# One kernel, one change: overflow rows of a block fetched one block ahead instead of two, held by a copy, and scattered when the block is closed

## The chip, the cores and the metric

The kernel runs on 1 core of one Trainium2 chip. The metric is the device time of one execution in microseconds (us). Before the change it is 3940.48 us, the median of 3 runs (3938.98 to 3941.68).

## The reference

A graph of 10000 nodes and 160000 edges, 128 features a node. Seven hops of a normalized sparse sum, then one small attention block over the eight tokens of each node:

```python
h = x                                            # (10000, 128)
toks = [x]
for _ in range(7):
    msg = h[src] * deg_inv_sqrt[src, None] * deg_inv_sqrt[dst, None]
    h = segment_sum(msg, dst, N)                 # sum over the edges into each node
    toks.append(h)
tok = stack(toks, axis=1)                        # (N, 8, D)
...                                              # layernorm, q/k/v, softmax, wo, layernorm, readout
```

The change touches only the hops.

## The kernel before, in words

The destination nodes lie in 79 blocks of 128. One hop is 79 blocks in a fixed order (the list `order`), and the hops follow each other. The table of the last hop's values, split in two f16 halves, lies on the chip (`tab`, 128 partitions by 80 by 256) and, row by row, in memory as well (`tabd` the whole table, `tabh` the last rows of it). For each block a tile `w` of zeros and ones in fp8 says which edge takes which source row and which destination it adds to. It is made once, in hop 1, and in hops 2 to 7 loaded from memory for every block.

A block of hops 2 to 7 works in three steps on TensorE (PE):

- *Gather* (line 608): 72 small matmuls with 128x32 weights out of `w` pick source rows out of `tab` into PSUM. They go in nine pairs of eight, each pair into one PSUM tile `p`, of which there are six. Each pair is then scaled by 4 and copied to an f16 tile `eb`, by ScalarE (ACT, line 613) for pairs 0, 2, 4, 5, 7 and by VectorE (DVE, line 615) for pairs 1, 3, 6, 8. This is called an evacuation below.
- *Scatter* (line 583, `scat`): 18 matmuls with 128x128 weights out of `w` add the nine `eb` tiles into the block's accumulator `acc`.
- Two more matmuls add rows that the gather does not hold. `og[n][0]` are 128 rows of `tabh` (the last group), `og[n][1]` are *overflow rows*, up to 128 edges that found no place in the cells of `w`; their destinations are in `Sov`. Both are brought from memory by an indirect DMA that GpSimd (POOL) issues (`fetch`, line 544). `begin` opens the accumulator with them (line 568), after the nine gathers of the block.

The matmuls of a block are not issued all at once. `pend` holds scatters that wait, with a lag of two: in block n, after the gathers and `begin`, PE does the last two scatters of block n-1, then the close of block n-1, and then the first seven scatters of block n. `close` reduces the accumulator on DVE (`s`, line 599), ACT and DVE then write the block's row of the next table (`entries`, lines 644 to 646), POOL scales the block's token (`r`, line 653), and the sync engine stores both.

The first two blocks of a hop cannot have their overflow rows when they begin, because those may come from any row of the table that the last hop has just finished. They are `late`: `begin` leaves the overflow matmul out, and `close` does it (line 597), behind the block's last scatter.

`ahead(n)` issues fetches from block n. In the normal case it is called just behind the block's first pair: it fetches `og[n+2][0]`, and this fetch is held by a one-column copy from that pair's `eb` tile to `og` (line 543), so that it doesn't start earlier; then it fetches `og[n+2][1]`, which has no copy of its own. At n = 0 the overflow rows of blocks 0, 1 and 2 are fetched together, at n = 1 those of block 3. Each of the two `og` tags has three buffers.

Of the kernel before, what the change touches and what calls it, by code (L numbers as in the profile page):

```python
# [19 lines left out]
NT = 79  # L20
NG = 18
NI = 1
# [25 lines left out]
class Hops:  # L48
# [608 lines left out]
    def run(self, ctx, att, nhop=K):  # L657
        tc, nc, V, A, T, G = self.tc, self.nc, self.nc.vector, self.nc.scalar, self.nc.tensor, self.nc.gpsimd
        with ExitStack() as c:
# [11 lines left out]
            pend = []  # L671
# [54 lines left out]
        with ExitStack() as c:  # L726
            lp = c.enter_context(tc.tile_pool(name="lp2", bufs=1))
            self.mx[0], self.ctok[1] = (lp.tile([128, NT], F32, name=z) for z in ("mx0", "ctok1"))
            self.c1 = [lp.tile([128, NT], F32, name=f"c1{i}") for i in range(2)]
            self.gsp = c.enter_context(tc.tile_pool(name="gs2", bufs=5))  # L730
            self.pg = c.enter_context(tc.tile_pool(name="pg2", bufs=6, space=PSUM))
            self.pacc = c.enter_context(tc.tile_pool(name="pc2", bufs=2, space=PSUM))
            self.ogp = c.enter_context(tc.tile_pool(name="og2", bufs=3))
            self.fp = c.enter_context(tc.tile_pool(name="fp2", bufs=4))
            self.sp = c.enter_context(tc.tile_pool(name="sp2", bufs=2))
            self.more_ebufs(c.enter_context(tc.tile_pool(name="eb2", bufs=1)), 9, False)
            pend = []
            for k in range(2, nhop + 1):
                i = 1 - k % 2
                tab, din = self.tab[i], (self.tabd[i], self.tabh[i])  # L740
                ct = self.ctok[i]
                last = k == nhop
                V.tensor_scalar(ct, self.disT, self.sinv, None, op0=ALU.mult)


                def scale(part, n, i=i, k=k):
                    if part == 0 and n == 0 and k == 2:
                        self.count()
                    if part != 1 - n:
                        return  # L750
                    if n == 0:
                        mc = self.sp.tile([128, 1], F32, name="mc")
                        V.tensor_reduce(mc, self.mx[i], axis=X, op=ALU.max)
                        scale.m = self.colmax(self.pg, self.sp, mc, "p")
                        V.tensor_mul(scale.m, scale.m, self.rho)
                    else:
                        q = self.pow2_of(self.pg, self.sp, scale.m, 2.0 ** 8, "p")
                        V.tensor_mul(self.sinv, self.sinv, q[:, 1:2])
                        V.tensor_scalar(self.c1[i], self.dis2, q[:, 0:1], None, op0=ALU.mult)

                def fin(t, s, acc, k=k, ct=ct, last=last, i=i):
                    if not last:
                        self.entries(t, s, i)
                        self.rows(1 - i, self.tab[1 - i], t, t + 1, nc.sync)
                    self.token_out(k, t, s, ct)


                order = [*range(4 * NG, NT), *range(4 * NG)]
                og = [[None] * (NI + 1) for _ in order]


                def ahead(n, after=None, og=og, order=order, din=din):
                    if n + 2 < NT:
                        for j in range(NI):
                            og[n + 2][j] = self.fetch(order[n + 2], j, din, after=None if j else after)
                    for m in range(0 if n == 0 else n + 2, min(n + 3, NT) if n >= 0 else 0):
                        og[m][NI] = self.fetch(order[m], NI, din, "ogl" if m < 2 else None)

                ahead(-2)
                ahead(-1)  # L780
                for n, t in enumerate(order):
                    w = self.gsp.tile([128, (NJ + NG) * 128], F8, name="w")
                    nc.sync.dma_start(w, self.GSd[t])
                    if k == 2 and n == 20:
                        att.constants(c, self.pg.tile([128, 512], F32, name="aw", tag="p"), self.ident)
                    if last and 40 <= n < 40 + 8 * FIRST:
                        att.load((n - 40) // 8, (n % 8,))

                    after = pend.pop() if n == 1 else None
                    for _ in self.block(t, w, tab, og[n], pend, 2, (9,), False, lambda jj: jj in (0, 2, 4, 5, 7), fin, n == 0, n < 2,  # L790
                                        (lambda part, n=n: scale(part, n)) if n < 2 and not last else None,
                                        lambda after=None, n=n: ahead(n, after), after):
                        pass
                while pend:
                    pend.pop(0)()
# [578 lines left out]
```

## Time and profile before

| | before |
|---|---|
| time, median of 3 runs | 3940.48 us |
| time of the profiled execution | 3935.55 us |
| its span, first to last instruction | 3933.8 us |
| mean granted TensorE clock | 0.977 |
| PE busy | 3693.9 us (94%) |
| DVE busy | 3172.3 us (81%) |
| ACT busy | 2812.9 us (72%) |
| POOL busy | 1678.8 us (43%) |

The profiled execution is 4.9 us under the median, and 1.75 us of it lie outside the span. Hops 2 to 7 lie from about 1170 us to 3282 us of the span.

How to read it: a row of the timeline gives the start in us, the busy time in us, the engine, the line, the operation, the tiles as out<-in, and how many instructions are merged (x). In square brackets stands the idle time of the engine just before it, and what ended that idle time. A matmul's start is recorded and its end is modelled, so an engine that waits for a matmul's result can wait longer than the matmul's row says. A row of the windows gives the stretch, its length, and then the busy time (and number of instructions) of PE, PE's weight loads, DVE, ACT and POOL in it, the granted clock, the DMA share and GB/s.

### The profile page before, as it was taken

Reading aid. Unit: us, or ns where it says so; the run is one execution under the profiler, and the core shown is the slowest. Engines: PE = TensorE matmul, PEld = TensorE weight load, DVE = VectorE, ACT = ScalarE, POOL = GpSimd, SP = SyncE. Lnnn points to the kernel's source line nnn. Section 1 sums busy time; section 2 is a strip of 40 time slices with the busy share of each in tenths; the row PEclk is TensorE's granted clock in tenths of the full one; section 3 lists DMA queues with packets and bytes.
Section 4 is the critical chain, followed back from the end, with each engine's and each line's share of the span. In section 5 each row is a group of like instructions: output and inputs, shape, how many; then the busy total and the mean of one; then the engine's idle time right before and its main releaser. Section 6 shows DMA issues by size and latency. Waiting matters only on the chain.

```text
span 3933.8 us, 174231 instructions
## 1 busy us (share of the span) xinstructions
PE 3693.9 (94%) x74141; PEld 2983.6 (76%) x74141; DVE 3172.3 (81%) x6888; ACT 2812.9 (72%) x6950; POOL 1678.8 (43%) x2221
## 2 busy tenths in 40 slices
PE   6786899999989999999999999999999998999997
PEld 4665677777768888888788788888878886777775
DVE  8998999999967777777777777777776664888888
ACT  6885577777766666766666667666765667888885
POOL 0000233323236665666666566656656662121111
PEclk8898899999999999999999999999999999999998
DMA  3100454544546666666666666666666552222220
GB/s 101 38 2 1 140 168 154 163 152 161 161 150 202 202 199 194 204 199 204 188 201 201 192 201 203 198 192 199 204 192 201 187 187 92 82 77 85 77 83 19
DMA packets 332729, 595.58 MB, mean 151 GB/s; under 512 B 57447, under 2 KB 215493, under 8 KB 326693
## 3 DMA queue, kind: packets, MB, share of 16 engines
q1 hardware_dynamic: 293989, 506.70, 40.0%
q0 software_dynamic: 35392, 72.55, 6.5%
q8 instruction: 580, 9.50, 1.0%
q10 hardware_dynamic: 2560, 5.12, 0.5%
q14 instruction: 208, 1.70, 0.1%
HBM read 455.49 MB, written 128.67 MB: 148 GB/s over the span
## 4 chain that ended last, share of the span: by engine, by line
PE 75%; DVE 14%; ACT 4%; DMA 4%; issue 2%; SPq 0%; another core or an unknown queue 0%; ACTq 0%; DVEq 0%; POOLq 0%
PE p L608 27%; PE acc L583 23%; PE acc L568 4%; PE pv L1018 4%; PE pu L1002 3%; DVE ux L226 2%; DVE o L219 2%; PE po L1037 2%; PE pt L992 2%; DVE oh L213 2%; PE tb L449 2%; DVE w L532 2%; PE ps L1067 1%; DVE R L219 1%; PE acc L558 1%
## 5 line engine op out<-in xcount | busy, mean ns | idle before, releaser
L613 ACT ACTIVATE eb<-p 128x512 f16<-128x512 f32 x3065 | 1638.7, 603 | 571.0 <-PE p L608 339.1
L615 DVE TENSOR_TENSOR eb<-p,four 128x512 f16<-128x512 f32 x1912 | 1230.9, 685 | 327.5 <-PE acc L583 189.7
L608 PE MATMUL p<-tab,w 128*32 128x256 f16 x39816 | 1291.8, 274 | 39.4 <-ACT eb L613 17.4
L608 PEld LDWEIGHTS <-w 128*32 128x32 fp8e4 x39816 | 997.5, 96 | 223.8 <-issue 169.2
L583 PE MATMUL acc<-eb,w 128*128 128x256 f16 x8532 | 1014.2, 273 | 0.5 <-issue 0.3
L583 PEld LDWEIGHTS <-w 128*128 128x128 fp8e4 x8532 | 836.9, 98 | 99.8 <-issue 1.0
L544 POOL DMA_INDIRECT og<-tabh,oidx x553 | 616.9, 1115 | 655.2 <-DVE oidx L468 394.5
L544 POOL DMA_INDIRECT og<-tabd,oidx x541 | 551.8, 1020 | 739.1 <-PE acc L566 359.6
L653 POOL TENSOR_SCALAR r<-s,ctok 128x128 f32<-128x128 f32 x474 | 294.8, 622 | 44.8 <-DVE s L599 27.8
L644 ACT ACTIVATE tab<-s,c 128x128 f16<-128x128 f32 x395 | 158.5, 401 | 198.0 <-DVE eb L615 171.4
L645 DVE SCALAR_TENSOR_TENSOR tab<-s,c,tab 128x128 f16<-128x128 f32 x395 | 138.9, 352 | 180.9 <-issue 168.3
L1107 POOL TENSOR_TENSOR p<-e,in 128x1024 f32<-128x1024 f32 (+1 forms) x40 | 76.5, 1914 | 446.6 <-DVE e L1106 446.6
L1059 ACT ACTIVATE junk<-tab 128x128 f32<-128x128 f32 x626 | 248.4, 401 | 8.2 <-SPq L1343 6.8
L347 ACT ACTIVATE rs<-iof,rb 128x128 fp8e4<-128x128 f32 x784 | 231.8, 391 | 0.3
L558 PE MATMUL acc<-eb,w 128*128 128x129 f16 x1422 | 214.2, 223 | 1.0 <-ACT w L529 0.9
L532 DVE TENSOR_TENSOR w<-dsl,iof 128x2432 fp8e4<-128x2432 f16 x79 | 211.9, 2682 | 2.7 <-PE acc L559 2.7
L599 DVE TENSOR_REDUCE s<-acc 128x128 f32<-128x256 f32 x474 | 196.3, 414 | 19.9 <-issue 8.9
L559 PE MATMUL acc<-eb,w 128*128 128x128 f16 x1422 | 210.1, 220 | 0.0
L543 POOL COPY og<-eb 128x1 f16<-128x1 f16 x452 | 84.0, 186 | 254.3 <-ACT eb L613 254.3
L558 PEld LDWEIGHTS <-w 128*128 128x128 fp8e4 x1501 | 139.2, 98 | 68.0 <-issue 64.3
L1018 PEld LDWEIGHTS pv<-Wv,xT 128*64 128x64 f32 x2504 | 138.8, 137 | 44.4 <-ACT uT L1003 29.7
L1018 PE MATMUL pv<-Wv,xT 128*64 128x131 f32 x2504 | 163.1, 280 | 8.6 <-issue 3.9
(299 smaller groups left out, 5033.1 us busy)
## 6 DMA issues: line engine op xcount, KB each, us to landing
w<-gsd SPq DMA_DIRECT2D x474, 592.0 KB
gsd<-w SPq DMA_DIRECT2D x79, 592.0 KB
tok<-r SPq DMA_DIRECT2D x546, 64.0 KB
tab<-tok SPq DMA_DIRECT2D x273, 128.0 KB
tabd<-tab SPq DMA_DIRECT2D x396, 64.0 KB
ra<-srow SPq DMA_DIRECT2D x79, 320.0 KB
rb<-srow SPq DMA_DIRECT2D x79, 256.0 KB
og<-tabh,oidx POOLq DMA_INDIRECT x553
```

The costliest lines, as they stand in the source:

```text
L347: A.activation(ro[:, j - a, i, :], self.iof, AF.Abs_reciprocal_sqrt, scale=2.0 ** 21, bias=rb[:, j - VP, i:i + 1], saturate=False)
L532: V.tensor_tensor(w[:, :NJ * 128].rearrange("p (j d) -> p j d", d=128), dsl[:, g, :, None].to_broadcast([128, NJ, 128]), self.iof1[:, None ...
L544: self.nc.gpsimd.indirect_dma_start(out=o, out_offset=None, in_=src[0] if i == NI else src[1], in_offset=bass.IndirectOffsetOnAxis(ap=self ...
L558: T.matmul(acc[0][:, :128 + ones], W, rows[:, 128:256 + ones], start=start, stop=False, skip_group_check=True)
L559: T.matmul(acc[0][:, :128], W, rows[:, :128], start=False, stop=False, skip_group_check=True)
L583: T.matmul(acc[0][:, :256], w[:, J * 128:(J + 1) * 128], e[:, j, :256], start=False, stop=J == NG - 1 and not late)
L608: T.matmul(p[32 * q:32 * q + 32, j], w[:, NJ * 128 + s * CAP:NJ * 128 + (s + 1) * CAP], tab[:, s, :], start=True, stop=True)
L613: A.activation(e[:, :n, 0:256], pv, AF.Copy, scale=4.0)
L615: V.tensor_tensor(e[:, :n, 0:256], pv, self.four[:, :, None].to_broadcast([128, n, 256]), op=ALU.mult)
L653: self.nc.gpsimd.tensor_scalar(r, s, ct[:, t:t + 1], None, op0=ALU.mult)
L1018: T.matmul(p[64 * h:64 * h + 64, u - us[0], :], S[i]["xT"][:, h * m + q, 64 * c:64 * c + 64], Wv, start=True, stop=True, tile_position=(0, ...
L1059: A.activation(j, S[i]["x"][:, g, :], AF.Square, bias=S[i]["x"][:, g, 0:1], scale=-1.0, accum_out=R[i % 6][:, 0, g:g + 1])
```

## The change

In hops 2 to 7 every block is now `late`: its overflow matmul stands in `close` and no longer in `begin`. The overflow rows of block n+1 are fetched in `ahead(n)`, from block 2 on, one block ahead and not two. This fetch too is held by a one-column copy of the block's first pair. At n = 0 the first three blocks' rows are fetched as before; at n = 1 no overflow rows are fetched.

```diff
                     if n + 2 < NT:
                         for j in range(NI):
                             og[n + 2][j] = self.fetch(order[n + 2], j, din, after=None if j else after)
-                    for m in range(0 if n == 0 else n + 2, min(n + 3, NT) if n >= 0 else 0):
-                        og[m][NI] = self.fetch(order[m], NI, din, "ogl" if m < 2 else None)
+                    if n == 0:
+                        for m in range(3):
+                            og[m][NI] = self.fetch(order[m], NI, din, "ogl" if m < 2 else None)
+                    elif 1 < n < NT - 1:
+                        og[n + 1][NI] = self.fetch(order[n + 1], NI, din, after=after)
...
-                    for _ in self.block(t, w, tab, og[n], pend, 2, (9,), False, lambda jj: jj in (0, 2, 4, 5, 7), fin, n == 0, n < 2,
+                    for _ in self.block(t, w, tab, og[n], pend, 2, (9,), False, lambda jj: jj in (0, 2, 4, 5, 7), fin, n == 0, True,
```

What this does to the order of the instructions shows on two engines. On PE, in a block in the middle of hop 2 (`og` the fetched rows, `Sov` the overflow destinations, `acc` the accumulators):

```order
 L568 LDWEIGHTS w
 L568 MATMUL acc<-og_24898,w 128x256
-L568 LDWEIGHTS Sov
-L568 MATMUL acc<-og_24901,Sov 128x256
 L583 LDWEIGHTS w
 L583 MATMUL acc<-eb_260,w 128x256
...
 L583 LDWEIGHTS w
 L583 MATMUL acc<-eb_262,w 128x256
+L597 LDWEIGHTS Sov
+L597 MATMUL acc<-og_24901,Sov 128x256
 L583 LDWEIGHTS w
 L583 MATMUL acc<-eb_264,w 128x256
```

The same weights and the same matmul stand four scatter matmuls later, for the block before, between the last scatter of that block and the first of the next. The number of instructions on PE is the same.

On POOL, two blocks in the middle of a hop, before (`og0` the last group's rows, `og1` the overflow rows, `r` the token):

```order
L543 COPY og0_43527<-eb12_24215 128x1
L544 DMA og0_43527<-tabh0_168,oidx_255 128x256
L544 DMA og1_43657<-tabd0_166,oidx_255 128x256
L653 TENSOR_SCALAR r_43625<-s_43619,ctok0_250 128x128
L543 COPY og0_43654<-eb7_24210 128x1
L544 DMA og0_43654<-tabh0_168,oidx_255 128x256
L544 DMA og1_43784<-tabd0_166,oidx_255 128x256
L653 TENSOR_SCALAR r_43752<-s_43746,ctok0_250 128x128
```

The scheduler that writes the order has moved the overflow fetch forward by a block: `og1_43657` is used by the same block as `og0_43654`, but its fetch stands one block earlier, beside that of `og0_43527`. It waits there for the buffer that the overflow matmul of the block in work gives back, so in fact overflow rows are asked for three blocks ahead.

Two such blocks in the changed kernel:

```order
L543 COPY og0_40342<-eb2_260 128x1
L543 COPY og1_40345<-eb2_260 128x1
L544 DMA og0_40342<-tabh0_168,oidx_255 128x256
L544 DMA og1_40345<-tabd0_166,oidx_255 128x256
L653 TENSOR_SCALAR r_40441<-s_40435,ctok0_250 128x128
L543 COPY og0_40470<-eb11_24214 128x1
L543 COPY og1_40473<-eb11_24214 128x1
L544 DMA og0_40470<-tabh0_168,oidx_255 128x256
L544 DMA og1_40473<-tabd0_166,oidx_255 128x256
L653 TENSOR_SCALAR r_40569<-s_40563,ctok0_250 128x128
```

Both copies stand ahead of both fetches, and the fetches follow each other with nothing between them. The copy of `og1` has taken over its fetch's wait for the buffer, which is now that of the block two before; the fetches wait only for their copies. POOL has 456 instructions more, one copy in each of 76 blocks of six hops.

On POOL at the start of hop 3, before (`ogl` the overflow rows of blocks 0 and 1):

```order
L544 DMA og0_34585<-tabh0_168,oidx_255 128x256
L544 DMA ogl_34452<-tabd0_166,oidx_255 128x256
L544 DMA ogl_34454<-tabd0_166,oidx_255 128x256
L544 DMA og1_34456<-tabd0_166,oidx_255 128x256
L544 DMA og1_34587<-tabd0_166,oidx_255 128x256
L544 DMA og1_34633<-tabd0_166,oidx_255 128x256
L653 TENSOR_SCALAR r_34615<-s_34608,ctok0_250 128x128
L543 COPY og0_34630<-eb12_24215 128x1
L544 DMA og0_34630<-tabh0_168,oidx_255 128x256
```

And in the changed kernel:

```order
L544 DMA og0_34661<-tabh0_168,oidx_255 128x256
L544 DMA ogl_34528<-tabd0_166,oidx_255 128x256
L544 DMA ogl_34530<-tabd0_166,oidx_255 128x256
L544 DMA og1_34532<-tabd0_166,oidx_255 128x256
L653 TENSOR_SCALAR r_34689<-s_34682,ctok0_250 128x128
L543 COPY og0_34704<-eb12_24215 128x1
L543 COPY og1_34707<-eb12_24215 128x1
L544 DMA og0_34704<-tabh0_168,oidx_255 128x256
L544 DMA og1_34707<-tabd0_166,oidx_255 128x256
```

Where five fetches from `tabd` stood in a row there are three; the other two now stand behind copies of block 2 and of block 3. On DVE and ACT the order is the same in both kernels.

## The prediction

> **What bounds the kernel now.** The page's first part was read first.
>
> ```profile
> PE 3693.9 (94%) x74141; PEld 2983.6 (76%) x74141; DVE 3172.3 (81%) x6888; ACT 2812.9 (72%) x6950; POOL 1678.8 (43%) x2221
> ```
>
> PE is busy 94% of the span, so next comes the timeline of one block in the middle of hop 4, to see whether anything but PE ends a block.
>
> ```profile
> 1800.94 2.15 PE L608 MATMUL p<-tab,w 128*32 128x256 f16 x72
> 1801.45 2.06 ACT L613 ACTIVATE eb<-p 128x512 f16<-128x512 f32 x4 [0.35 <-PE p L608]
> 1802.11 0.18 POOL L543 COPY og<-eb 128x1 f16<-128x1 f16 x1 [0.55 <-ACT eb L613]
> 1802.57 1.02 POOL L544 DMA_INDIRECT og<-tabh,oidx  x1 [0.27 <-POOL og L543]
> 1803.02 0.28 PE L568 MATMUL acc<-og,w 128*128 128x256 f16 x1
> 1803.14 0.27 PE L568 MATMUL acc<-og,Sov 128*128 128x256 f16 x1
> 1803.25 2.13 PE L583 MATMUL acc<-eb,w 128*128 128x256 f16 x18
> 1803.98 0.60 ACT L613 ACTIVATE eb<-p 128x512 f16<-128x512 f32 x1 [0.46 <-PE acc L583]
> 1804.01 0.69 DVE L615 TENSOR_TENSOR eb<-p,four 128x512 f16<-128x512 f32 x1 [0.45 <-PE acc L583]
> 1804.32 0.95 POOL L544 DMA_INDIRECT og<-tabd,oidx  x1 [0.72 <-PE acc L583]
> 1804.62 0.41 DVE L599 TENSOR_REDUCE s<-acc 128x128 f32<-128x256 f32 x1
> 1805.07 0.40 ACT L644 ACTIVATE tab<-s,c 128x128 f16<-128x128 f32 x1 [0.49 <-DVE eb L615]
> 1805.30 0.62 POOL L653 TENSOR_SCALAR r<-s,ctok 128x128 f32<-128x128 f32 x1
> 1805.31 2.15 PE L608 MATMUL p<-tab,w 128*32 128x256 f16 x72
> 1805.50 0.35 DVE L645 SCALAR_TENSOR_TENSOR tab<-s,c,tab 128x128 f16<-128x128 f32 x1 [0.47 <-issue]
> 1806.05 1.89 DVE L615 TENSOR_TENSOR eb<-p,four 128x512 f16<-128x512 f32 x3
> ```
>
> The block runs from 1800.94 to 1805.31, 4.37 us, and PE has no bracket in it: it never waits. Call the start T. Two evacuations, the eighth on ACT (T+3.04) and the ninth on DVE (T+3.07), come late: all 72 gathers ended at 1803.09 by their row, T+2.15, and both engines were idle 0.46 and 0.45 us. The name in the bracket, a scatter matmul, isn't what they need. What lies over that time on another engine is the `tabh` fetch on POOL, T+1.63 to T+2.65. The waits over hops 2 to 7 say that this is the rule:
>
> ```profile
> ACT eb L613 <- PE acc L583: 189.5, 406, 0.8
> DVE eb L615 <- PE acc L583: 188.6, 418, 0.8
> ```
>
> Some 410 of 474 blocks show it, with 0.46 us each. I read it so: while POOL issues an indirect fetch, and 0.3 to 0.4 us beyond, a matmul's signal reaches ACT and DVE late. PE itself goes on; it suffers only when its six buffers `p` are full. That point is near: the ninth evacuation, the reduce (T+3.68), lines 644 and 645 and then the next block's first DVE evacuation stand in one queue. The latter starts at 1806.05 and its first of three takes a third of 1.89, so it ends near 1806.7; the next block's eighth pair, which reuses its buffer, starts at 1805.31 plus seven ninths of 2.15, 1806.98. With the signal's way back the slack is 0.1 to 0.25 us.
>
> The Trainium skill speaks against my reading: "SBUF — State Buffer", section "Who interferes with whom", says that only the port pair which VectorE and GpSimd share causes contention, and that TensorE and ScalarE never wait on anyone. The row of 406 waits on ACT does not look so; what the time would be by that rule is the last rival.
>
> The blocks that are longer stand at the hops' starts. The windows of the third block of hops 3 to 7 (length, PE, PE loads, DVE, ACT, POOL, clock, DMA share, GB/s), with a normal block ahead:
>
> ```profile
> 1800.94:1805.31 4.37, 4.37 (x95) 3.71 (x94) 3.45 (x7) 3.07 (x7) 2.79 (x5) 1.00 0.65 200
> 1527.11:1533.21 6.10, 5.22 (x94) 3.83 (x93) 3.69 (x8) 3.33 (x7) 3.49 (x5) 1.00 0.33 73
> 1876.13:1887.57 11.44, 8.48 (x94) 5.24 (x93) 4.33 (x10) 3.35 (x7) 5.71 (x8) 0.70 0.43 124
> 2231.62:2239.78 8.16, 5.88 (x95) 3.96 (x95) 4.39 (x10) 3.35 (x7) 5.16 (x7) 1.00 0.37 104
> 2584.23:2594.21 9.98, 7.20 (x95) 4.68 (x95) 4.42 (x10) 3.24 (x7) 5.76 (x8) 0.83 0.49 145
> 2941.01:2947.73 6.72, 6.28 (x94) 4.30 (x93) 3.52 (x6) 2.88 (x5) 4.97 (x8) 0.75 0.24 65
> ```
>
> Over 4.37 us they lose 1.73, 7.07, 3.79, 5.61 and 2.35, together 20.6 us. The timeline of hop 4 shows why:
>
> ```profile
> 1873.16 0.95 POOL L544 DMA_INDIRECT ogl<-tabd,oidx  x1 [2.43 <-DMA tabd<-tab]
> 1875.94 0.27 PE L597 MATMUL acc<-ogl,Sov 128*128 128x256 f16 x1
> 1878.16 0.94 POOL L544 DMA_INDIRECT og<-tabd,oidx  x1 [0.30 <-issue]
> 1881.77 0.69 DVE L615 TENSOR_TENSOR eb<-p,four 128x512 f16<-128x512 f32 x1 [4.65 <-remote]
> ```
>
> Five fetches start between 1873.16 and 1878.16, 1.25 us apart, and DVE is idle 4.65 us until 1881.77, after gathers that had long run.
>
> **The change part by part.** *The moved matmul.* One matmul of the overflow form, 1803.02 to 1803.14, so 0.11 us from start to start, moves four scatters later on PE. The sum for PE is zero. The close now holds it, but it was ahead of the close before too, so the reduce's input is ready at the same time. Nothing covers this; nothing needs to.
>
> *When the rows must be there.* The fetch now starts near T+3.1 and its matmul stands after two blocks, the gathers, line 568 and four scatters: 2×4.37 + 2.08 + 5×0.11 = T+11.4, 8.3 us later. The first fetch of hop 4 started at 1873.16 and its rows were used at 1875.94, so 2.8 us do. Cost zero, unless a fetch takes three times that. What is queued behind the new copy on POOL is both fetches and the token `r`; for `r` waits only the sync engine's store, and nobody on PE.
>
> *The second copy.* 456 copies of 0.18 us. POOL works 2.79 us of 4.37 us in the windows row, so its own time is covered. But both copies stand ahead of both fetches, so the `tabh` fetch moves from T+1.63 by 0 to 0.24 us (the lower end if the 0.27 us ahead of it covers the copy, the upper with 0.06 us for the step between two); I take 0.18, T+1.81. The eighth pair's signal is then due before the hold begins and its evacuation is on time.
>
> *The second fetch.* Before, it waited 0.72 us for a buffer that the block's own overflow matmul gives back, T+3.38. Now that wait has been met long ago (the buffer is that of two blocks before), so it starts 0.30 us behind the first, T+3.13: back to back in each block. The close's last matmul is issued near T+2.6, its signal due at T+2.8 or so, inside the first fetch's hold. The nearest rows are the few blocks of before in which the two fetches happen to stand so:
>
> ```profile
> 1535.39 1.02 POOL L544 DMA_INDIRECT og<-tabh,oidx  x1 [0.51 <-POOL og L543]
> 1536.72 0.96 POOL L544 DMA_INDIRECT og<-tabd,oidx  x1 [0.30 <-PE acc L583]
> 1536.76 0.42 DVE L599 TENSOR_REDUCE s<-acc 128x128 f32<-128x256 f32 x1 [0.21 <-PE acc L583]
> ...
> 1539.77 1.02 POOL L544 DMA_INDIRECT og<-tabh,oidx  x1 [0.51 <-POOL og L543]
> 1541.10 0.95 POOL L544 DMA_INDIRECT og<-tabd,oidx  x1 [0.30 <-issue]
> 1541.81 0.42 DVE L599 TENSOR_REDUCE s<-acc 128x128 f32<-128x256 f32 x1 [0.75 <-PE acc L583]
> ```
>
> In the first the reduce starts 1.37 us after the first fetch, in the second 2.04 us. From T+1.81 that gives the reduce at T+3.18 or T+3.85, against T+3.68 now. I take the first: early, no cost. The price of the second is the first rival. A third row, of the start of hop 5, is far worse and is the second rival. A gain is excluded here, since the block is PE's 4.37 us already.
>
> *The hop's start.* Five fetches in a row become three. They start 1.25 us apart, and DVE resumes 8.6 us after the first of five, 1.72 us for each. With three, signals come free some 3.75 to 5.2 us after the first fetch, near 1876.9 to 1878.3, while the six buffers are full six ninths of 2.15 us after 1876.13, at 1877.56. With half a microsecond for the first evacuation PE loses 0 to 1.3 us. I take 1.3 for each of the five hops, the high end, as the two fetches taken out come back as a back-to-back pair with block 2. Gain: 20.6 − 5×1.3 = 14 us; ends 10 (half the stall stays) and 20.6 (all goes).
>
> Sum: 0 + 0 + 0 − 14. On the profiled execution (3935.55 us, 4.9 under the median) that is 3921.5; on the median 3940.5 − 14 = 3926.
>
> **The rivals.** *The reduce is held a little* (as at 1539.77). It comes at T+3.85 to T+4.0 where T+3.68 has 0.1 to 0.25 us of slack, so 0.06 to 0.2 us of stall, and the block that followed those two shows it:
>
> ```profile
> 1542.18:1546.74 4.56, 4.55 (x94) 3.71 (x93) 3.41 (x8) 3.42 (x7) 2.89 (x5) 1.00 0.88 217
> ```
>
> 4.56 is 0.19 us more than 4.37. A block that stalls moves its signals later against the fetches, so I count every second of 385 blocks (five hops of 77; the last hop writes no table and has no such queue): 192 × 0.06 to 0.19 = 12 to 37 us, net of the 14 from −2 to +23. It gives about 3946. For it: one of two rows. Against it: the other.
>
> *The reduce is held until the second fetch is over.* This ends slower. The row at the start of hop 5:
>
> ```profile
> 2244.23 1.02 POOL L544 DMA_INDIRECT og<-tabh,oidx  x1 [3.09 <-issue]
> 2245.55 0.96 POOL L544 DMA_INDIRECT og<-tabd,oidx  x1 [0.30 <-PE p L608]
> 2247.11 1.89 DVE L615 TENSOR_TENSOR eb<-p,four 128x512 f16<-128x512 f32 x3 [0.89 <-PE p L608]
> ```
>
> Here evacuations whose gathers fell into the first fetch resume 2.8 to 2.9 us after its start. The reduce would come at T+1.81+2.8 = T+4.6, 0.93 late. The queue on ACT and DVE hands nearly all of it to the next block's first evacuations, so PE stalls some 0.85 us. If every second block does, 192 × 0.85 = 163 us, net +149: 4089. If each did, 327. It decides from the point where the reduce comes later than T+3.9 on average. For it: it is the only row with several signals inside the first hold, and there is at least one more ahead of the close. Against it: in the two rows above, the signals lie nearest to where the change puts them.
>
> *The hold has nothing to do with fetches.* By the page named above, evacuations wait for something else at a hop's start, such as the arrival of rows, and fetches moved on POOL leave the stall. Then the normal blocks stay at 4.37 us and the third blocks at 6 to 11 us: 3940.5. Against it stand the idle 4.65 us beside matmuls of 1876.13 that needed none of those rows.
>
> **How the numbers follow.** A measurement of this kernel can tell 0.2%, 7.9 us, from no change. My forecast has a chance of 0.41, its own range 3918 to 3932 (a gain of 8 to 22, the ends above with 2 us of the difference between executions). The small hold has 0.20, the long hold 0.34, no effect 0.05. The range must reach the long hold, since without it 0.34 is left out: 3916 to 4090; its own upper half, beyond every second block, is left out. Faster: the forecast but for its upper edge, and a tenth of the small hold, 0.42. Same: no effect, that edge, and half of the small hold, 0.17. Slower: the long hold and the rest, 0.41.
>
> **What would show it right or wrong.** Right: third blocks of hops 3 to 7 of 5 to 6 us; normal blocks of 4.37; the `tabh` fetch at T+1.8 and the `tabd` fetch 1.3 us later; the eighth evacuation at T+2.1 and the reduce near T+3.2. Wrong: PE rows of gathers (L608) with idle time in every second block, and a reduce at T+3.85 (small hold) or T+4.6 (long hold). If third blocks stay at 6 to 11 us, the reason for the stall is not the row of fetches. If PE waits at line 597 for `og`, the rows land too late and the second part is wrong.

## The result, and the profile after

| | before | after |
|---|---|---|
| time, median of 4 runs | 3941.08 us | 3997.40 us |
| time of the profiled execution | 3935.55 us | 3999.36 us |
| its span | 3933.8 us | 3997.6 us |

The changed kernel is slower: ratio 1.0143, 95% interval 1.0126 to 1.0161. Both were measured on one chip, called the first chip here (its number is not known; it may be the chip 2 of below). On another chip (7) the change made no difference, as the experiments show.

Among the waits of hops 2 to 7 after the change (window 1190 to 3280; us in total, times, longest) the two evacuation rows of some 410 each are all but gone. These three rows name the late overflow matmul (line 597) as what ended the wait:

```profile
DVE s L599 <- PE acc L597: 170.9, 327, 5.3
DVE eb L615 <- PE acc L597: 27.6, 52, 1.5
ACT eb L613 <- PE acc L597: 4.9, 5, 1.2
```

The eighth and ninth evacuations seldom wait any more. The reduce does, 327 times, 0.52 us in the mean. The timeline of one block in hop 3, with the start of the next:

```profile
1827.48 2.25 PE L608 MATMUL p<-tab,w 128*32 128x256 f16 x72
1828.66 0.31 POOL L543 COPY og<-eb 128x1 f16<-128x1 f16 x2 [0.52 <-ACT eb L613]
1829.39 1.02 POOL L544 DMA_INDIRECT og<-tabh,oidx  x1 [0.43 <-POOL og L543]
1830.22 0.27 PE L597 MATMUL acc<-og,Sov 128*128 128x256 f16 x1
1830.72 0.96 POOL L544 DMA_INDIRECT og<-tabd,oidx  x1 [0.30 <-issue]
1831.49 0.42 DVE L599 TENSOR_REDUCE s<-acc 128x128 f32<-128x256 f32 x1 [0.64 <-PE acc L597]
1831.94 0.40 ACT L644 ACTIVATE tab<-s,c 128x128 f16<-128x128 f32 x1 [1.40 <-issue]
1831.95 1.10 PEld L608 LDWEIGHTS <-w 128*32 128x32 fp8e4 x44 [0.21 <-issue]
```

T, the block's start, is 1827.48. The first fetch starts at T+1.91, the second at T+3.24, 0.30 us behind the first one's end. The last matmul of the close starts at T+2.74; the reduce that needs it starts at T+4.01, 2.10 us after the first fetch's start. The block is 4.47 us long, and the gathers take 2.25 us where they took 2.15: PE waits for a buffer near their end.

Not all blocks look so. In hop 4:

```profile
2133.15 0.95 POOL L544 DMA_INDIRECT og<-tabd,oidx  x1 [0.30 <-DMA tabd<-tab]
2134.19 2.22 PE L608 MATMUL p<-tab,w 128*32 128x256 f16 x72
2134.88 2.56 ACT L613 ACTIVATE eb<-p 128x512 f16<-128x512 f32 x5 [0.82 <-PE p L608]
2136.27 1.02 POOL L544 DMA_INDIRECT og<-tabh,oidx  x1 [0.43 <-POOL og L543]
2137.65 0.42 DVE L599 TENSOR_REDUCE s<-acc 128x128 f32<-128x256 f32 x1 [0.18 <-PE acc L597]
```

Here the reduce is early, 1.38 us after the first fetch. But the first evacuation of the block starts at T+0.69 and not at T+0.51: its matmuls' signal comes late, and what lies ahead of it is the second fetch of the block before, which ends only 0.09 us ahead of T. With it the copies and the first fetch move to T+2.08, and the second fetch again lies late enough to do the same to the next block. So one such block follows another.

Of the 402 blocks with n (the place in the hop) from 10 to 76, counted in the trace, 218 have the reduce at T+3.8 or later (median 2.13 us after the first fetch) and lose 39.7 us against 4.368 us each; the other 184 (1.37 us) lose 20.8 us. Of the 402, 37 are still 4.38 us or shorter. By place, against 4.368 us for each block:

| us over 4.368 a block, hops 2 to 7 | before | after |
|---|---|---|
| first two blocks | 16.5 | 14.3 |
| third block | 20.9 | 6.8 |
| n = 3 to 9 | 3.3 | 18.8 |
| n = 10 to 76 | 9.2 | 60.6 |
| last two | 2.6 | 10.4 |

The sum is 58.4 us more, of 63.8 us between the two spans. The third blocks are the gain (windows of hops 3 to 7, same columns as in the prediction):

```profile
1548.42:1554.74 6.32, 6.25 (x93) 4.71 (x92) 3.82 (x8) 3.07 (x6) 2.89 (x5) 0.73 0.30 71
1909.96:1915.40 5.44, 4.92 (x93) 3.65 (x93) 4.24 (x11) 2.84 (x6) 3.09 (x6) 1.00 0.59 176
2270.88:2276.05 5.17, 4.81 (x94) 3.61 (x94) 2.92 (x7) 2.84 (x6) 3.11 (x6) 1.00 0.48 155
2633.77:2639.35 5.58, 5.06 (x94) 3.69 (x93) 3.79 (x8) 2.84 (x7) 3.37 (x6) 1.00 0.70 189
2998.84:3004.83 5.99, 5.99 (x94) 4.54 (x93) 3.32 (x6) 2.99 (x5) 2.86 (x5) 0.72 0.24 52
```

### The profile page after: what moved, and what is told of

Its sections match the earlier page's. It is cut to its first block, busy times and chain, and to the rows that moved or that the text cites. A ratio compares the mean times of both kernels' runs of the same rounds, so it can differ in the third digit from the quotient of the medians.

```text
span 3997.6 us, 174696 instructions
## 1 busy us (share of the span) xinstructions
PE 3753.7 (94%) x74141; PEld 2988.3 (75%) x74141; DVE 3157.0 (79%) x6888; ACT 2769.4 (69%) x6950; POOL 1755.2 (44%) x2677
## 3 DMA queue, kind: packets, MB, share of 16 engines
q1 hardware_dynamic: 293989, 506.70, 39.7%
## 4 chain that ended last, share of the span: by engine, by line
PE 62%; DVE 4%; issue 2%; ACT 2%; DMA 1%; POOL 0%; SPq 0%; another core or an unknown queue 0%; POOLq 0%; DVEq 0%; ACTq 0%
PE p L608 23%; PE acc L583 21%; PE pv L1021 4%; PE pu L1005 3%; PE acc L568 2%; DVE eb L615 2%; PE po L1040 2%; PE pt L995 2%; PE acc L597 1%; PE ps L1070 1%; PE pf L1229 1%; PE sm L1076 1%; DMA og<-tabd,oidx 1%; ACT tab L644 0%; ACT junk L1062 0%
## 5 line engine op out<-in xcount | busy, mean ns | idle before, releaser
L613 ACT ACTIVATE eb<-p 128x512 f16<-128x512 f32 x3065 | 1595.1, 606 | 425.0 <-PE p L608 379.9
L608 PE MATMUL p<-tab,w 128*32 128x256 f16 x39816 | 1345.3, 275 | 47.1 <-ACT eb L613 16.4
L615 DVE TENSOR_TENSOR eb<-p,four 128x512 f16<-128x512 f32 x1912 | 1195.2, 682 | 234.9 <-PE p L608 168.6
L583 PE MATMUL acc<-eb,w 128*128 128x256 f16 x8532 | 1060.9, 273 | 0.1
L653 POOL TENSOR_SCALAR r<-s,ctok 128x128 f32<-128x128 f32 x474 | 306.5, 647 | 149.7 <-issue 87.1
L543 POOL COPY og<-eb 128x1 f16<-128x1 f16 x908 | 141.4, 182 | 266.2 <-ACT eb L613 264.5
```

What stands on the lines that cost most here:

```text
L583: T.matmul(acc[0][:, :256], w[:, J * 128:(J + 1) * 128], e[:, j, :256], start=False, stop=J == NG - 1 and not late)
L608: T.matmul(p[32 * q:32 * q + 32, j], w[:, NJ * 128 + s * CAP:NJ * 128 + (s + 1) * CAP], tab[:, s, :], start=True, stop=True)
L613: A.activation(e[:, :n, 0:256], pv, AF.Copy, scale=4.0)
L615: V.tensor_tensor(e[:, :n, 0:256], pv, self.four[:, :, None].to_broadcast([128, n, 256]), op=ALU.mult)
L653: self.nc.gpsimd.tensor_scalar(r, s, ct[:, t:t + 1], None, op0=ALU.mult)
```

## The experiments

**One part at a time, on chip 5.** Theory P: the two fetches, 0.30 us apart, make the close's signal late. Rivals: L, that the late overflow matmul does it, and C, that the copy does it by moving the first fetch. The edits, against the kernel before for the first three and against the changed kernel for the last (the line that calls `ahead2` is new, its definition is left out here):

```diff
 e1_late_alone
-  ..., fin, n == 0, n < 2,
+  ..., fin, n == 0, True,
 e2_two_copies
   self.nc.gpsimd.tensor_copy(o[:, 0:1], after)
+  self.nc.gpsimd.tensor_copy(o[:, 1:2], after)
 e3_copy_alone
-  og[m][NI] = self.fetch(order[m], NI, din, "ogl" if m < 2 else None)
+  og[m][NI] = self.fetch(order[m], NI, din, "ogl" if m < 2 else None, after if n > 1 else None)
 e4_last_pair_holds (the overflow fetch is called from the block's pair 8)
-  elif 1 < n < NT - 1:
-      og[n + 1][NI] = self.fetch(order[n + 1], NI, din, after=after)
+  if jj == 8 and ahead2:
+      ahead2(self.ebuf[(self.eb_i - 1) % len(self.ebuf)][:, 0, 0:1])
```

> Every block closes with its overflow matmul (late), but the rows are fetched as in the kernel before, without a copy; five fetches from the table still stand in a row at a hop's start. Theory P (two fetches 0.30 us apart hold the close's signal and the next block's first one): the overflow fetch still waits for a buffer, so it starts at T+3.3 to T+3.5, normal blocks stay at 4.37 us and the total within 8 us of before (3933 to 3949). Theory L (the overflow matmul in the close makes the reduce late): normal blocks 4.45 to 4.5 us, total 3975 to 4000. Theory C (the copy that moves the first fetch later): as P, since no copy is added.

> The kernel before, with a second one-column copy ahead of each held tabh fetch, so that this fetch starts some 0.3 us later; the overflow fetch keeps its wait for a buffer. Theory P: the second fetch still starts 0.5 us or more behind the first one's end, normal blocks 4.37 us, total 3936 to 3950. Theory C: normal blocks 4.45 to 4.5 us, total 3975 to 4000. Theory L: as before, 3941.

> The overflow rows are fetched two blocks ahead as in the kernel before and their matmul opens the block, but from block 2 on the fetch is held by a copy of the block's first pair; four fetches in a row at a hop's start. Theory P: the second fetch follows the first by 0.30 us, normal blocks 4.43 to 4.5 us as in the changed kernel, the third blocks of hops between those of before and of the change, total 3985 to 4005. Theory L: normal blocks 4.37 us, total 3930 to 3940. Theory C: as P.

> The changed kernel, with the overflow fetch held by the block's last pair and not by its first: its copy then stands behind the tabh fetch, and the second fetch starts near T+3.5 and not at T+3.24. Theory P: normal blocks back at 4.37 us, third blocks of hops as in the changed kernel (6.8 us over 4.37 in all), total 3922 to 3932, faster than both kernels. Theory L: normal blocks 4.45 to 4.5 us, total 3985 to 4000. Theory C: 4.37 us, since only one copy stands ahead of the first fetch.

Measured against the kernel before on the same chip (3910.28 us): e1 0.9989 (0.9976 to 1.0002), e2 0.9990 (0.9977 to 1.0004), e3 0.9994 (0.9982 to 1.0006), e4 0.9987 (0.9975 to 0.9999). Normal blocks were 4.37 us in all four, the copy alone included, where P expected 4.43 to 4.5. So nothing is told apart, theory C by e2 as little (its second copy moved the fetch by 0.13 us, to T+1.76, and not by 0.3). But the kernel before is 31 us faster here than on the first chip, and its signals are on time. So the next question was the chip.

**The two kernels on another chip (7).** Theory H: signals are held on some chips and not on others. Theory K: it is the kernel.

> The kernel before, unchanged, for its profile on the chip of this call. In the four runs so far the eighth and ninth evacuations came at T+2.44 and T+2.55 beside the tabh fetch, where the first profile of this kernel has T+3.04 and T+3.07, and the kernel before took 3910 us, not 3941. Theory H (whether matmul signals are held while POOL issues a fetch belongs to the chip that the program ran on, not to the program): on a chip that holds, T+3.04 and 3941 us; on one that does not, T+2.44 and 3910 us, with no idle time in the third blocks of hops. Theory K (it belongs to these kernels' fetch order): T+3.04 on either.

> The changed kernel, unchanged, beside the one before on the same chip. Theory H: on a chip that holds, 1.2 to 1.6% slower with normal blocks of 4.43 to 4.5 us; on one that does not, normal blocks of 4.37 us and a total within 0.2% of before. Theory K: 1.2 to 1.6% slower on either.

> The copy alone, as e3_copy_alone. On a chip that holds: theory P (two fetches 0.30 us apart) 4.43 to 4.5 us for normal blocks and 1 to 1.6% slower; theory L (the late matmul) 4.37 us and within 0.3% of before. On a chip that does not hold: 4.37 us, within 0.2%, as it was.

> The change with the overflow fetch held by the last pair, as e4_last_pair_holds. On a chip that holds: theory P 4.37 us for normal blocks, third blocks of hops as in the changed kernel, 0.2 to 0.5% faster than before; theory L 4.45 to 4.5 us and 1 to 1.5% slower. On a chip that does not hold: 4.37 us, within 0.2% of before.

The change makes no difference there: 1.0000 (0.9989 to 1.0011), at 3910.18 us beside 3910.39; the kernel before against itself gives 0.9995 (0.9983 to 1.0007). The copy alone gives 0.9995 (0.9985 to 1.0004), the last pair's 0.9989 (0.9979 to 0.9999). The timeline of the kernel before on this chip:

```profile
1817.95 2.15 PE L608 MATMUL p<-tab,w 128*32 128x256 f16 x72
1818.46 2.56 ACT L613 ACTIVATE eb<-p 128x512 f16<-128x512 f32 x5 [0.89 <-PE p L608]
1818.69 2.48 DVE L615 TENSOR_TENSOR eb<-p,four 128x512 f16<-128x512 f32 x4 [0.46 <-PE p L608]
1819.58 1.02 POOL L544 DMA_INDIRECT og<-tabh,oidx  x1 [0.27 <-POOL og L543]
1820.90 0.95 POOL L544 DMA_INDIRECT og<-tabd,oidx  x1 [0.30 <-DMA tabd<-tab]
1821.09 0.41 DVE L599 TENSOR_REDUCE s<-acc 128x128 f32<-128x256 f32 x1
```

The same program, the same fetch at T+1.63: now five evacuations of ACT and four of DVE run without a gap, and the reduce comes at T+3.14. The second fetch is back to back with the first here too, since the signal it waits for is on time, and delays nothing. The changed kernel has the same picture, with the reduce 1.23 us after the first fetch:

```profile
1820.91 1.02 POOL L544 DMA_INDIRECT og<-tabh,oidx  x1 [0.43 <-POOL og L543]
1822.14 0.41 DVE L599 TENSOR_REDUCE s<-acc 128x128 f32<-128x256 f32 x1
1822.23 0.95 POOL L544 DMA_INDIRECT og<-tabd,oidx  x1 [0.30 <-issue]
```

The trace also records when each of PE's semaphore updates, its signals, was made. In the 402 blocks n = 10 to 76 of the kernel before on the first chip, 10 updates lie between 0.2 and 1.2 us after the start of the `tabh` fetch and 1953 in the 0.4 us behind; with the same program on chip 7 it is 1195 and 383. In the block at 1800.94 that the prediction shows, the updates of the five matmuls that start between 1802.60 and 1803.57 all stand between 1803.90 and 1804.12. So it is PE's signal itself that comes late, and not the engine that waits for it.

The third blocks of the kernel before lose 6.2 us in six hops here, not 20.9. K falls, and H fits. But each of the numbered chips was measured in one session only, so whether it is the chip, or something else that stayed the same within a session, is not told apart.

**What a late reduce costs, without a hold (chip 13).** Two and three reduces in a close, in the changed kernel, put the result late on a chip that holds nothing.

```diff
-  V.tensor_reduce(s, acc[0][:, 0:256]...)
+  for _ in range(2):      # three in g2
+      V.tensor_reduce(s, acc[0][:, 0:256]...)
```

> The changed kernel with the reduce of the accumulator done twice in each close, so that its result comes some 0.45 us later. This stands in for a held signal on a chip that does not hold: the last reduce starts near T+3.6, as late as in the kernel before on the first chip (T+3.68). Theory Q (the price of a late reduce is the queue lines 599, 644, 645 and the next block's first evacuations, with 0.1 to 0.25 us of slack after T+3.68): normal blocks 4.37 us, total within 0.2% of before. Theory R (the length of blocks after the change comes from elsewhere): 4.37 us as well. On a chip that holds: 4.8 us or more.

> The same with three reduces; the last one starts near T+4.05, as late as in the changed kernel on the first chip (T+4.0). Theory Q: normal blocks of hops 2 to 6 get 0.08 to 0.2 us longer, 4.45 to 4.57 us, those of hop 7 stay at 4.37, total 0.8 to 2% slower than before. Theory R: 4.37 us, within 0.2%. On a chip that holds: over 5 us.

> The copy alone, for the case that this call's chip holds signals: then theory P (two fetches 0.30 us apart) 4.43 to 4.5 us for normal blocks, theory L (the late matmul) 4.37 us. On a chip that does not hold, 4.37 us, as twice before.

> The overflow fetch held by the last pair, for the case that this call's chip holds signals: then theory P 4.37 us for normal blocks and 0.2 to 0.5% faster than before, theory L 4.45 to 4.5 us. On a chip that does not hold, 4.37 us, as twice before.

With two reduces 0.9987 (0.9974 to 1.0000) and 4.37 us a block; with three 1.0272 (1.0254 to 1.0290), 4.66 us in hops 2 to 6 and 4.37 in hop 7, which writes no table. The reduce rows of g1 and g2, each with the next block's gathers:

```profile
1830.47 0.88 DVE L600 TENSOR_REDUCE s<-acc 128x128 f32<-128x256 f32 x2
1831.70 2.15 PE L609 MATMUL p<-tab,w 128*32 128x256 f16 x72
```

```profile
1831.60 1.34 DVE L600 TENSOR_REDUCE s<-acc 128x128 f32<-128x256 f32 x3
1832.78 2.44 PE L609 MATMUL p<-tab,w 128*32 128x256 f16 x72
```

An end 0.35 us ahead of the next block's start costs nothing; 0.16 us behind it costs 0.29 us a block. On the first chip the kernel before ended it 0.28 us ahead (1805.03, 1805.31) at no cost, the changed kernel 0.04 us ahead (1831.91, 1831.95) at 0.10 us. Between the two that cost, 0.20 us later costs 0.19 us. So the lateness of the reduce is enough to explain the longer blocks of its kind (218 of 402); Q stands for these. g2 also missed its size: 2.7% and 0.29 us, not up to 2% and 0.2. The copy alone gave 1.0001 (0.9990 to 1.0012), the last pair's fetch 0.9986 (0.9974 to 0.9997).

**The parts on a chip that holds (2).** One execution of each; before took 3937.31 us there.

> The changed kernel, a look at its profile on one more chip. If matmul signals arrive late there during POOL's fetches (the two in question at T+3.0 or later in any kernel of this call), normal blocks are 4.43 to 4.5 us; if not, 4.37 us.

> The copy alone. On a chip that holds signals: 4.43 to 4.5 us by theory P (two fetches 0.30 us apart), 4.37 us by theory L (the late matmul). On one that does not: 4.37 us.

> The late matmul alone, fetches as before. On a chip that holds signals: 4.37 us by theory P, 4.43 to 4.5 us by theory L. On one that does not: 4.37 us.

> The change with the overflow fetch held by the last pair. On a chip that holds signals: 4.37 us and third blocks as in the changed kernel by theory P, 4.43 to 4.5 us by theory L. On one that does not: 4.37 us.

This chip holds signals. These are single executions, and 31 of the kernel before on chip 7 span 25 us, so the block lengths count for more here than the totals. The change took 3977.69 us, the copy alone 3971.30, the late matmul alone 3934.01, the last pair's fetch 4056.87. The copy alone gives 34 of the change's 40 us. It has the changed kernel's reduce, 2.09 us after the fetch, and 323 of its 402 blocks n = 10 to 76 are longer than 4.38 us. Two blocks, one of 4.37 and the next of 4.56 us (the timeline of the first, then the windows of both):

```profile
1860.56 1.02 POOL L544 DMA_INDIRECT og<-tabh,oidx  x1 [0.42 <-POOL og L543]
1861.88 0.94 POOL L544 DMA_INDIRECT og<-tabd,oidx  x1 [0.30 <-DMA tabd<-tab]
1862.65 0.42 DVE L599 TENSOR_REDUCE s<-acc 128x128 f32<-128x256 f32 x1 [0.77 <-PE acc L583]
```

```profile
1858.65:1863.02 4.37, 4.37 (x95) 3.71 (x94) 3.13 (x7) 2.56 (x5) 2.74 (x5) 1.00 0.67 193
1863.02:1867.58 4.56, 4.55 (x94) 3.71 (x93) 3.41 (x8) 3.02 (x7) 2.89 (x6) 1.00 0.74 186
```

The late matmul alone keeps the fetch's wait, on line 597 now, and looks like the kernel before (timeline, then the window of the block):

```profile
1906.67 0.60 ACT L613 ACTIVATE eb<-p 128x512 f16<-128x512 f32 x1 [0.47 <-PE acc L597]
1907.04 0.96 POOL L544 DMA_INDIRECT og<-tabd,oidx  x1 [0.76 <-PE acc L597]
1907.31 0.41 DVE L599 TENSOR_REDUCE s<-acc 128x128 f32<-128x256 f32 x1
```

```profile
1903.62:1907.99 4.37, 4.37 (x94) 3.70 (x93) 3.45 (x7) 3.06 (x7) 2.78 (x5) 1.00 0.70 218
```

So it is the copy, and L falls. The copy does two things, though: it moves the first fetch 0.28 us (theory C) and it frees the second of its wait (theory P). e2, meant to part them, ran on a chip that does not hold, where the second fetch's wait is short anyway. What speaks for P is in the traces. In the kernel before, where the second fetch starts 0.72 us behind the first one's end, the two held evacuations came 1.41 and 1.44 us after the first fetch's start; here, with 0.30 us, the reduce came only after 2.09. And a few blocks have the first fetch as late as the copy puts it, but not the second one close behind. This is one in hop 4 of the kernel before on the first chip (it starts at 1891.94, so the first fetch is at T+1.94):

```profile
1893.88 1.02 POOL L544 DMA_INDIRECT og<-tabh,oidx  x1 [0.52 <-POOL og L543]
1895.27 0.42 DVE L599 TENSOR_REDUCE s<-acc 128x128 f32<-128x256 f32 x1
1895.44 0.94 POOL L544 DMA_INDIRECT og<-tabd,oidx  x1 [0.54 <-PE acc L583]
```

The reduce comes 1.39 us after the first fetch. In five traces of the two chips that hold (the kernel before and the change on the first, the change, the copy alone and the late matmul alone on chip 2) 509 blocks (n from 3 to 76) have the first fetch between T+1.88 and T+1.98 and the ninth evacuation on time. Where the second fetch starts less than 1.5 us behind the first one's start, the reduce comes more than 1.7 us after it in 470 of 503; in the six others (two of the kernel before, four of the copy alone) it comes after 1.39 to 1.45 us. So the later first fetch alone does not make the reduce late, as far as six blocks can show it.

P's own cure fails too: with the last pair's copy the second fetch starts later than expected, after the reduce, and comes into the next block:

```profile
1857.24 0.98 POOL L544 DMA_INDIRECT og<-tabd,oidx  x1 [0.27 <-DMA tabd<-tab]
1857.51 0.60 DVE L647 SCALAR_TENSOR_TENSOR tab<-s,c,tab 128x128 f16<-128x128 f32 x1 [0.47 <-ACT tab L646]
1857.56 1.71 PE L608 MATMUL p<-tab,w 128*32 128x256 f16 x56
1858.67 2.70 DVE L615 TENSOR_TENSOR eb<-p,four 128x512 f16<-128x512 f32 x4 [0.36 <-PE p L608]
```

DVE is free at 1858.31 and waits 0.36 us more for the second pair's signal, until 1.43 us after the fetch's start; the normal block becomes 4.67 us, in hop 7 too. What counts is not the distance of the fetches alone, but whether a signal that somebody waits for falls under either. Third blocks on this chip lose 5.4 and 6.9 us with three fetches in a row, 18.4 with four, 23.7 with five.

**The wait given back by fewer buffers (chip 8).** The changed kernel without the second copy, and one or two buffers for the overflow rows.

```diff
-  og[n + 1][NI] = self.fetch(order[n + 1], NI, din, after=after)
+  og[n + 1][NI] = self.fetch(order[n + 1], NI, din)     # og1: 1 buffer (k1), 2 buffers (k2)
```

> The changed kernel without the second copy and with one buffer for the overflow rows in hops 2 to 7 (not three), so that the overflow fetch again waits for a matmul of the block in work (line 597) and only three fetches from the table stand in a row at a hop's start. On a chip that holds signals: the fetch starts at T+3.3 to T+3.4, normal blocks 4.37 us, third blocks as in the changed kernel, 0.2 to 0.5% faster than before by theory P; were the copies or the late matmul the cause, 4.37 and 4.45 us. On a chip that does not hold: 4.37 us, within 0.2% of before. If one buffer is too few, PE waits at line 597 for the rows.

> The same with two buffers: four fetches in a row at a hop's start, the wait for a matmul of the block in work kept. On a chip that holds signals: normal blocks 4.37 us, third blocks between the changed kernel's and those of before, 0.1 to 0.4% faster than before. On a chip that does not hold: 4.37 us, within 0.2% of before.

One buffer: 1.0460 (1.0443 to 1.0478). PE waits for the rows, `PE acc L597 <- DMA og<-tabd,oidx` 152 times, 146.7 us in all:

```profile
1854.86 0.94 POOL L544 DMA_INDIRECT og<-tabd,oidx  x1 [0.95 <-PE acc L597]
1859.70 0.27 PE L597 MATMUL acc<-og,Sov 128*128 128x256 f16 x1 [1.01 <-DMA og<-tabd,oidx]
```

Two buffers: 3901.72 us beside 3907.23, ratio 0.9982 (0.9972 to 0.9992), a gain of 0.2% and within the noise the same as the last pair's fetch (0.9986 to 0.9989 on three chips). This chip did not hold either (the nine evacuations run without a gap), so whether two buffers also beat the kernel before on a chip that holds is open.

## Why the prediction was wrong, point by point

It forecast 3926 us, faster; it is 3997.4 us, slower.

- *The step that failed is the second fetch, "I take the first: early, no cost".* Of the two rows at hand, 1.37 and 2.04 us, the second was the rule: 2.13 us in 218 of 402 blocks. Even the first was not free: in the other 184 blocks the reduce was early and the second fetch held the next block's first evacuation, which the prediction did not price at all.
- *The first rival named the mechanism and was mis-sized.* Its price per block, 0.06 to 0.19 us, holds (the median block is 4.47 us for 4.37). Its count, every second of 385 blocks, doesn't: nine blocks in ten are long, in hop 7 too, where the reduce hands nothing on and the next block's first evacuation is the one held. The range of −2 to +23 us became +56. Dearer than that price were also the blocks n = 3 to 9 (15.5 us in 42 blocks) and the last two (7.8 us in 12), where three fetches stand in a row ahead of the next hop. The rival's 3946 us stands on the profiled execution; on the median the middle of its range is 3951.
- *"A block that stalls moves its signals later against the fetches"* holds in stretches only: long and short blocks in turn, as in the two of the copy alone (4.37 and 4.56), are not the rule there either. Mostly the first fetch moved along.
- *The long hold* (reduce at T+4.6) did not come as a rule; 7 of 402 blocks have the reduce later than T+4.5.
- *The second copy: 0 to 0.24 us.* It moved the first fetch by 0.28 us, to T+1.91. That the eighth evacuation would then be on time was right.
- *The hop's start: −14 us.* Third blocks of hops 3 to 7 went from 20.6 to 6.7 us over 4.37, 13.9 us less. That the sum fits so well is in part luck: two of the five still lose 1.95 and 1.62 us, with PE busy all but throughout at a granted clock of 0.73 and 0.72, and that is no stall of the kind that was summed.
- *The moved matmul: zero.* Shown by the late matmul alone, 4.37 us a block.
- *"2.8 us do" for the rows.* Not tested by the change itself, which leaves 8.3 us; with one buffer a fetch of 1854.86 was used at 1859.70, 4.8 us later, with PE waiting. The bound of 2.8 us was too low for that place.
- *"The hold has nothing to do with fetches"* had 0.05. On chips that hold, moving the fetches moves the waits: evacuations (before), reduce (the change, the copy alone), the next block's second pair (last pair's fetch). On chip 7, which doesn't, its result is the measured one: no change. The Trainium skill's "SBUF — State Buffer", section "Who interferes with whom", says that TensorE and ScalarE never wait on anyone; it speaks of the ports to SBUF. The 406 evacuations of ACT that waited 189.5 us on the first chip waited for late signals of PE, so these runs neither bear it out nor refute it, and it was no rule to forecast this time by.

What makes the first chip and chip 2 hold signals is not shown; no run here looked into that. Nor did a run of its own part theories P and C: the six blocks above do.

## What to carry to other kernels

A wait that seems to be waste can keep an operation in the one quiet place of a period: before moving or freeing it, list which signals fall under its new place, those of the next period as well. A resource wait (here a buffer given back by the block's own matmul) follows the work when that is late; a copy tied to the start of the block does not. And a difference of 1% that hangs on signal times should be measured on more than one chip.

## What the runs showed of the hardware

- On the first chip and on chip 2 a matmul's signal came late beside an indirect fetch that POOL issues: in the kernel before on the first chip 10 of PE's semaphore updates lay between 0.2 and 1.2 us after the fetch's start and 1953 in the 0.4 us behind (chip 7: 1195 and 383). Evacuations ready by T+2.15 started 1.41 and 1.44 us after the fetch's start at T+1.63, and with a second fetch 0.30 us behind the first one's end the reduce started, in 218 of 402 blocks, some 2.1 us after the first one's start. On chips 5, 7, 8 and 13 the same instructions showed no delay, and the kernel before took 3907 to 3910 us, not 3937 to 3941.
- A two-input DVE operation (line 645, line 647 in that kernel) took 0.58 us in the mean where an indirect fetch is issued beside it (last pair's fetch, chip 2; 0.57 us on chip 7) and 0.35 us in the kernel before on the first chip (0.43 us on chip 7, where a fetch is seldom beside it).
